# Five changes at once in a layer's forward and backward pass: the filter's transform, the D term, column tiles, the order of the start and of the stage boundaries

## Chip, cores and metric

One core of a Trainium2 chip. The metric is the device time of one execution in microseconds (us). Medians are quoted with their lowest and highest run. Profiles are of single executions.

## The reference, cut to what matters

One layer over a sequence of 2048 rows of 1024 channels, all in bf16, and its gradients with regard to nine inputs:

```python
def _A_ref(q, k, v, shift_k, ssm_k, ssm_D):
    ...                                   # k_shift: 4-tap causal filter of k along the sequence
    kv = k_shift * v
    ...                                   # zero-padded to 4096 rows
    y_f = kv_f * kf_f                     # spectra of kv and of the long filter ssm_k
    y = irfft(y_f)[:S]                    # the long convolution
    y = y + kv * ssm_D                    # the D term
    return q * y

def _B_ref(x, w_gate, w_up, w_down):
    return ((x @ w_gate) * (x @ w_up)) @ w_down      # 1024 -> 3584 -> 1024

xn = layernorm(x)
out = x + _A_ref(xn, k, v, ...) * silu(_B_ref(xn, ...))
# outputs: out, and the vector-Jacobian products for x, k, v, shift_k, ssm_k, ssm_D, w_gate, w_up, w_down
```

## The kernel before

TensorE does the matrix products and also the convolution's Fourier transforms, as products with tables of 128 x 128. The convolution runs beside the big products: it is a generator of small steps ("units of work") that a pump advances after each block of the big products. There are six stages: layer norm (with the first two weight slabs); gate/up products with the forward convolution; bilinear output with the gate; dh and dWgate/dWup with the backward convolution; dWdown; dx with the gradient of k (dk).

The filter's transform took four tables and 64 matmuls per block of 128 channels, and the D term was added in time (two passes of VectorE over a block):

```python
    def fwd2(x, X, wp, psp):                    # radix 2: 4 x 2 x (4 x 2) matmuls of 256 columns
        for q in range(4):
            psS = psp.tile([P, 2, 256], F32, name="psS")
            psP = psp.tile([P, 2, 256], F32, name="psP")
            cmm(psS, T4[q], x, (0, 2, 4, 6))
            cmm(psP, T4[q], x, (1, 3, 5, 7))
            ...
            tt(X[:, 2 * q:2 * q + 2, :], s[:], psP[:], ADD)
            tt(X[:, 2 * q + 8:2 * q + 10, :], s[:], psP[:], SUB)
    ...
        def main(ds):                           # one block of 128 channels, forward
            ...
            yield from fwd4(kvs, KX, cs, ps_cv)             # kv already in radix 4
            yield from fwd2(S_["hx"], HX, cs, ps_cv)        # the filter
            tt(kvD[:], kvs, Dbc[...], MUL)                  # D term
            yield from product(KX, HX, KX, cs, False, 0)
            yield from inv_dft(KX, HX, cs)
        def tail(ds):
            ...                                             # 4 x inv_rows, ScalarE copies to yf
            tt(yf[:], yf[:], kvD[:], ADD)
```

The gradients of D and of the short filter need only the diagonal of a product, and took the whole product:

```python
            for b in range(NB):                 # D: 16 matmuls of 128 columns
                nc.tensor.matmul(ps[:, 0, :], x[:, b, :], kv[:, b, :], ...)
    ...
            for r in range(8):                  # dk: 8 matmuls of 512 columns, twice per channel block
                nc.tensor.matmul(ps[...], dk[:, r, :], kh[:, r:r + 4, :], ...)
```

The start, PSUM shares of the fourth stage, and its first lines:

```python
    slabs = [load_slab(0, nc.scalar)[0]]
    chunks = [(0, 2), (2, 2), (4, 4), (8, 4), (12, 4)]      # row blocks normed together
    ...
    ps_b = pool("ps_b", 4, space=PSUM)      # dh and dW
    ps_c3 = pool("ps_c3", 1, space=PSUM)    # transforms of dy
    ps_y = pool("ps_y3", 2, space=PSUM)     # rows of the inverse transforms
    ...
    flush()                                 # the gate's last transposes of dbm, ahead of dh
    first = dh_half(0, wdt)
```

Who issues what will matter: SyncE issues most loads, among them the transposed ones (`wdt`, `dgut`, the gate and up weights); ScalarE issues the stores of dWgate, dWup (`out_dram<-wb`) and of `DGd`, and it is also the engine that copies dh and dW out of PSUM (`dht`, `wb`); GpSimd issues the convolution's transfers.

## Time and profile before

| | kernel before |
|---|---|
| time, three runs | 2095.99 us (2095.94 to 2096.73) |
| span of its profile | 2084.4 us |
| TensorE busy | 96% |
| VectorE busy | 70%; 89% in the fourth stage |

The execution that was profiled took 2086.3 us, 10 less than the three runs. In a line of waits, the first name is the engine that waited and the group it then ran, after the arrow stands what ended the wait, then the sum in us, the number of times and the longest. In a timeline line the columns are start, length, engine, line, operation, tiles, count, and in brackets the idle time just before with its cause; "ACTq" and "SPq" are the issuing of a transfer by ScalarE and SyncE.

### The profile page before, as it was taken

The page shows a single profiled execution, that of the slowest core. Times are in us where ns is not written, and L with a number is a line of the kernel's source. Part 1 is how long each engine was busy: PE and PEld are TensorE (multiplying, and loading weights), DVE is VectorE, ACT ScalarE, POOL GpSimd, SP SyncE. Part 2 cuts the span into 40 slices and gives each one's busy share as a digit, 9 for nine tenths or more (in the row PEclk, how much of TensorE's full clock was granted, in tenths as well). Part 3 has the DMA queues.
Part 4 walks back from the last instruction along what each step waited for, and adds up shares of the span by engine and source line. Part 5 has one row for each costly group of instructions (what it writes and reads, how often), then busy time and mean ns, then how long its engine had stood idle before and what let it go on. Part 6 is the DMA issues. An engine that isn't in the chain of part 4 may idle for free.

```text
span 2084.4 us, 28857 instructions
## 1 busy us (share of the span) xinstructions
PE 2001.6 (96%) x11438; PEld 1088.1 (52%) x11626; DVE 1464.0 (70%) x1937; ACT 626.5 (30%) x969; POOL 339.9 (16%) x496
## 2 busy tenths in 40 slices
PE   7989999999999998999899999999999989999998
PEld 3455555555544446666556555565444434444443
DVE  7689898878726555787799999999697024344433
ACT  6734444444423333232122222222222101111112
POOL 3322222121112111000112212111121001110100
PEclk9999999999999999999999999999999999999999
DMA  8776676566598779666878888857954999393921
GB/s 292 241 256 205 220 234 250 186 214 241 178 309 271 246 239 322 212 209 162 257 232 273 242 221 263 246 199 248 253 196 145 236 191 221 96 211 91 225 69 57
DMA packets 454279, 451.29 MB, mean 217 GB/s; under 512 B 236944, under 2 KB 380600, under 8 KB 439680
## 3 DMA queue, kind: packets, MB, share of 16 engines
q1 hardware_dynamic: 308096, 185.89, 34.4%
q0 software_dynamic: 45120, 189.08, 26.8%
q10 hardware_dynamic: 100928, 74.47, 11.7%
q8 instruction: 91, 1.49, 0.3%
q14 instruction: 44, 0.36, 0.1%
HBM read 208.15 MB, written 194.02 MB: 193 GB/s over the span
## 4 chain that ended last, share of the span: by engine, by line
PE 42%; DVE 9%; issue 6%; DMA 2%; SPq 2%; POOL 1%; ACT 0%; another core or an unknown queue 0%; ACTq 0%; DVEq 0%; POOLq 0%
PE psx L1212 17%; PE psb L1101 9%; PE psb L1181 9%; PE psb L1082 4%; DVE W L199 3%; DVE m L199 2%; SPq L1152 1%; PE psdk L939 1%; DVE U L199 1%; DMA dyl<-DYd 1%; DMA B<-HFd 1%; DVE B L199 1%; PE psY L904 1%; DVE B L242 0%; SPq L1206 0%
## 5 line engine op out<-in xcount | busy, mean ns | idle before, releaser
L1101 PE MATMUL psb<-U,U 128*128 128x512 bf16 x1746 | 400.4, 383 | 9.5 <-ACT dht L1084 4.2
L567 PE MATMUL psg<-wslab,U 128*128 128x512 bf16 x1729 | 402.5, 380 | 4.2 <-ACT gut L569 0.7
L1212 PE MATMUL psx<-U,dgut 128*128 128x512 bf16 x1508 | 336.2, 380 | 7.4 <-DMA dgut<-DGd 5.8
L1212 PEld LDWEIGHTS <-dgut 128*128 128x128 bf16 x1792 | 175.5, 98 | 219.2 <-DMA dgut<-DGd 7.2
L1101 PEld LDWEIGHTS <-U 128*128 128x128 bf16 x1792 | 176.6, 99 | 210.2 <-issue 15.9
L567 PEld LDWEIGHTS <-U 128*128 128x128 bf16 x1792 | 173.4, 98 | 187.3 <-issue 4.6
L1082 PE MATMUL psb<-wdt,U 128*128 128x256 bf16 x1792 | 205.5, 274 | 0.0
L569 ACT CAST gut<-psg 128x512 bf16<-128x512 f32 x224 | 130.9, 585 | 218.6 <-PE psg L567 215.8
L1181 PE MATMUL psb<-U,U 128*128 128x512 bf16 x875 | 194.9, 379 | 1.1
L1082 PEld LDWEIGHTS <-U 128*128 128x128 bf16 x1792 | 176.2, 98 | 23.1
L964 PE MATMUL psbm<-U,ht 128*128 128x512 bf16 x766 | 170.4, 379 | 1.4 <-DMA ht<-HTd 0.4
L1105 ACT CAST wb<-psb 128x512 bf16<-128x512 f32 x112 | 65.5, 585 | 324.0 <-PE psb L1101 236.9
L199 DVE TENSOR_TENSOR W<-W 128x1024 f32<-128x1024 f32 (+1 forms) x144 | 146.1, 1033 | 2.7
L199 DVE TENSOR_TENSOR m<-A,B 128x1024 bf16<-128x1024 bf16 (+1 forms) x160 | 116.6, 791 | 37.2 <-issue 21.6
L1181 PEld LDWEIGHTS <-U 128*128 128x128 bf16 x896 | 87.0, 98 | 102.1
L1235 ACT ACTIVATE dx_t<-dxn 128x1024 bf16<-128x1024 f32 (+1 forms) x17 | 17.1, 1007 | 362.0 <-DVE dxn L199 310.8
L964 PEld LDWEIGHTS <-ht 128*128 128x128 bf16 x784 | 76.0, 98 | 89.7 <-DMA ht<-HTd 0.9
L199 DVE TENSOR_TENSOR dka<-dkh,Wbc 128x1024 bf16<-128x1024 bf16 x16 | 11.1, 692 | 156.6 <-DMA dkh<-DKSHd 156.6
L1084 ACT CAST dht<-psb 128x512 bf16<-128x512 f32 x112 | 65.1, 587 | 144.8 <-PE psb L1082 102.7
L199 DVE TENSOR_TENSOR U<-U,dht 128x2048 bf16<-128x2048 bf16 x56 | 71.6, 1282 | 18.5 <-ACT dht L1084 18.5
L1183 ACT CAST U<-psb 128x512 bf16<-128x512 f32 x56 | 32.8, 585 | 159.8 <-PE psb L1181 131.2
L199 DVE TENSOR_TENSOR gg<-bm,sig 128x1024 bf16<-128x1024 bf16 x16 | 11.1, 691 | 92.0 <-ACT sig L982 92.0
(239 smaller groups left out, 2473.9 us busy)
## 6 DMA issues: line engine op xcount, KB each, us to landing
U<-GUd SPq DMA_DIRECT2D x28, 1024.0 KB, 7.4
DGd<-U ACTq DMA_DIRECT2D x56, 512.0 KB, 5.7
GUd<-gut ACTq DMA_DIRECT2D x54, 512.0 KB, 4.6
A<-DYFd POOLq DMA_DIRECT2D x16, 1024.0 KB, 7.5
U<-Hd SPq DMA_DIRECT2D x15, 1024.0 KB, 6.1
out_dram<-wb ACTq DMA_DIRECT2D x224, 64.0 KB, 2.9
Hd<-hN POOLq DMA_DIRECT2D x54, 256.0 KB, 4.6
HTd<-hT POOLq DMA_DIRECT2D x54, 256.0 KB, 3.6
```

Of the source, the lines that this page charges most:

```text
L199: V.tensor_tensor(o, a, b, op)
L567: gu_mm[0] = nc.tensor.matmul(ps[:], XNT[q][:, dc, qi * P:(qi + 1) * P], w[:, dc].rearrange("p a f -> p (a f)"), start=(dc == 0), stop=(dc ...
L569: nc.scalar.copy(out=gut[:, i].rearrange("p a f -> p (a f)"), in_=ps[:])
L904: nc.tensor.matmul(ps[:, i, :], G[:, 2 * r + k, c * P:(c + 1) * P], TI[:, 0, r, k, :], start=(k == 0), stop=(k == 1))
L964: nc.tensor.matmul(ps[:, dh * 512:(dh + 1) * 512], ht(fc)[:, i * P:(i + 1) * P], WD[fc // 4][:, fc % 4, dh * 512:(dh + 1) * 512], start=(f ...
L1082: nc.tensor.matmul(ps[:, x * SLW:(x + 1) * SLW], DBMT[2 * hf + g][:, dc, (b % 4) * P:(b % 4 + 1) * P], wdt[:, dc, :], start=(dc == 0), sto ...
L1084: nc.scalar.copy(out=dht[:, 2 * e:2 * e + 2].rearrange("p b f -> p (b f)"), in_=ps[:])
L1101: nc.tensor.matmul(ps[:], XN[b // 4][:, b % 4, dc * P:(dc + 1) * P], dgus[b // 8][:, b % 8].rearrange("p a f -> p (a f)"), start=(b == 0), ...
L1105: nc.scalar.copy(out=wb[:].rearrange("p a f -> p (a f)"), in_=ps[:])
L1181: nc.tensor.matmul(ps[:], h[:, b, f * P:(f + 1) * P], DBM[b // 4][:, b % 4, dh * 512:(dh + 1) * 512], start=(b == 0), stop=(b == NB - 1))
L1183: nc.scalar.copy(out=wbs[:, dh * 512:(dh + 1) * 512], in_=ps[:])
L1212: nc.tensor.matmul(ps[:, dh * 512:(dh + 1) * 512], t[n][:, f, i * P:(i + 1) * P], WGU[n][:, f, dh * 512:(dh + 1) * 512], start=(n == 0 and ...
```

## The change

Its intent is to take work off TensorE (filter transform in radix 4: 32 matmuls in place of 64; diagonals by two column tiles of 64), work off VectorE (the D term becomes one small addition to the filter's spectrum; its passes in the forward and backward tails go), and holes off the boundaries (smaller first chunks; the last transposes of dbm behind the first dh half; transposed tiles for dx loaded during dWdown). Cut to its core:

```diff
-    T4 = [TF[:, 0], TF[:, 1], TFO[:, 0], TFO[:, 1]]
+    T4 = [TF[:, 0], TF[:, 1]]
...
-            yield from fwd2(S_["hx"], HX, cs, ps_cv)
+            yield from fwd4(S_["hx"], HX, cs, ps_cv)
             turned(HX, 1, 0, 1)
+            h0 = cv(HX[:])[:, :, 0, 0]
+            tt(h0, h0, Dbc[:, ds * P:(ds + 1) * P].unsqueeze(1).to_broadcast([P, 8, P]), ADD)
-            tt(kvD[:], kvs, Dbc[...].to_broadcast([P, NB, P]), MUL)
...
-            tt(yf[:], yf[:], kvD[:], ADD)
...                                    (W gets a second buffer in the forward pass)
-            flush(2)
+            flush(3)                   (transposes of hN one row block later)
...
-    slabs = [load_slab(0, nc.scalar)[0]]
-    chunks = [(0, 2), (2, 2), (4, 4), (8, 4), (12, 4)]
+    chunks = [(0, 1), (1, 1), (2, 2), (4, 4), (8, 4), (12, 4)]
...                                    (slab 0 on SyncE's queue, behind the first chunk)
-                nc.tensor.matmul(ps[:, 0, :], x[:, b, :], kv[:, b, :], ...)
+                for j in (slice(0, 64), slice(64, 128)):
+                    nc.tensor.matmul(ps[j, 0, 0:64], x[:, b, j], kv[:, b, j], ...)
...
-        tt(dy[:], dy[:], Dbc[...], MUL)
-        tt(y[:], y[:], dy[:], ADD)
...
-                nc.tensor.matmul(ps[:]..., dk[:, r, :], kh[:, r:r + 4, :]..., ...)
+                for j in (slice(0, 64), slice(64, 128)):
+                    nc.tensor.matmul(ps[j], dk[:, r, j], kh[:, r:r + 4, j], ...)
...
-    C_TOTAL = ... + 8 * 5.4 + 8 * 0.5     (pace of the backward convolution)
+    C_TOTAL = ... + 8 * 2.9 + 8 * 0.5
...
-    ps_b = ... 4;  ps_c3 = ... 1;  ps_y = ... 2
+    ps_b = ... 3;  ps_y = ... 1;  ps_c3 = ... 2, replaced by ps_y4 = ... 4 after the dy transforms
...
-    flush()
+    for e in later:
+        e[0] = -2
...
-    HSL = (3, 11, 6, 2)                   (tiles of h in dWdown: four)
+    HSL = (3, 11, 6)                      (three)
...                                    (nine weight tiles, as before, and now nine dgut tiles loaded during dWdown)
```

## The prediction

> **What bounds the kernel now.** I read the busy table first, then busy time by stretch (the stages cut where the big matmul groups begin and end), then the waits of each stretch. The columns of a stretch are its length, then busy time and instruction count of TensorE, its weight loads, VectorE, ScalarE and GpSimd, then clock and DMA.
>
> ```profile
> PE 2001.6 (96%) x11438; PEld 1088.1 (52%) x11626; DVE 1464.0 (70%) x1937; ACT 626.5 (30%) x969; POOL 339.9 (16%) x496
> ```
> ```profile
> 0.00:93.00 93.00, 78.90 (x490) 39.93 (x500) 67.09 (x158) 64.81 (x91) 28.55 (x51) 1.00 0.78 259
> 93.00:584.00 491.00, 472.96 (x3003) 278.32 (x3055) 408.65 (x518) 224.56 (x351) 107.51 (x163) 1.00 0.66 223
> 584.00:790.00 206.00, 200.32 (x1004) 94.52 (x1024) 106.41 (x168) 63.99 (x64) 39.35 (x62) 1.00 0.85 273
> 790.00:1450.00 660.00, 633.08 (x4026) 390.72 (x4073) 586.60 (x730) 172.34 (x302) 99.10 (x142) 0.98 0.77 235
> 1450.00:1653.00 203.00, 201.78 (x1039) 96.76 (x1058) 131.06 (x151) 42.74 (x77) 26.98 (x18) 1.00 0.82 207
> 1653.00:2084.40 431.40, 414.53 (x1882) 187.80 (x1918) 164.15 (x214) 58.08 (x86) 38.41 (x61) 0.99 0.65 149
> ```
>
> The reader is to see six stages (layer norm; gate/up products with the forward convolution; bilinear output with the gate; dh and dWgate/dWup with the backward convolution; dWdown; dx with dk) and TensorE near full in all. VectorE has room except in the fourth stage and, at 83%, the second. So TensorE bounds the time, and anything taken off it counts, unless VectorE steps in.
>
> The chain of waits shows that the busy matmuls are at their own rate:
>
> ```profile
> 1713.39 10.74 PE psx L1212 x49
> ```
>
> (10.74 - 0.38)/48 = 0.216 us from start to start, 0.38 being the last one's own duration in the table of groups. Time can therefore only come from fewer columns streamed or from the holes. The holes that concern the change:
>
> ```profile
> PE psb L1003 <- DVE dbm L199: 6.7, 1, 6.7
> PE psY L407 <- DVE B L199: 4.3, 1, 4.3
> PE psb L1101 <- ACT dht L1084: 4.2, 1, 4.2
> PE psY L407 <- ACT yl L882: 3.8, 1, 3.8
> ...
> PE psx L1212 <- DMA dgut<-DGd: 5.8, 3, 3.5
> ```
>
> The first four are in the fourth stage (the first is its very beginning), the last is the start of dx.
>
> **What the Trainium skill says.** "TensorE: Matmul & The Clock Gate", section "Back-to-back issue gap": a warm matmul of N columns follows the last after N/2.4 + 2.5 ns: 215.8, 109.2 and 55.8 ns for 512, 256 and 128. The trace agrees (0.216 us above; runs of 128-column transposes start 0.056 us apart). "TensorEngine Tiling (Array Packing)", section "Key Properties": column tiles work in parallel, but a change of tiling mode drains the array; its section "Restrictions" says column tiling turns the fast weight load off. The kernel before never tiles, so no trace here shows either. "VectorE: DVE Perf Modes", section "Side-by-side": two-input 16-bit operations reach two results a cycle, fp32 one; the trace agrees: 512 fp32 elements take 682 ns, 1024 bf16 elements 682 ns.
>
> **The change part by part.**
>
> (1) *Filter transform in radix 4, D in the spectrum.* The old transform of the filter takes 64 matmuls of 256 columns for each of 8 column blocks, the new one 32, as the transform of kv has. Removed: 256 x 0.1092 = 28.0 us of TensorE, all in stage 2. VectorE pays. Its groups (union of time, 8 blocks):
>
> ```profile
> L199 DVE TENSOR_TENSOR HX<-Ws,psP 128x512 bf16<-128x512 f32 x64 | 40.8, 682 | 20.2 <-PE psP L216 20.1
> L199 DVE TENSOR_TENSOR W<-W,psP 128x512 f32<-128x512 f32 x64 | 40.4, 682 | 14.7 <-ACT W L229 13.8 <-PE psP L216 0.6
> L199 DVE TENSOR_TENSOR KX<-W 128x512 bf16<-128x512 f32 x64 | 39.8, 683 | 0.0
> L199 DVE TENSOR_TENSOR kvD<-kv,Dbc 128x2048 bf16<-128x2048 bf16 x8 | 9.8, 1224 | 0.2
> L199 DVE TENSOR_TENSOR yf<-yf,kvD 128x2048 bf16<-128x2048 bf16 x8 | 9.8, 1222 | 18.2 <-ACT yf L670 18.0
> ```
>
> The first row goes, a second copy of rows two and three comes: +80.2 - 40.8 = +39.4. Rows four and five go: -19.6. The new addition of D to the spectrum is 8 operations of 1024 bf16, 0.64 each: +5.1. Net +24.9 us. Now the stage by its two engines. TensorE ideal before: 1536 products of 512 columns x 0.2158 + 512 transposes x 0.0558 + 1024 of kv, filter and inverse x 0.1092 = 472, against 491 measured; after: 444. VectorE before had 405 of its 409 us done when the last block's inverse ended, at 565.6; TensorE had waited 1.4 us for it there and needed 20 us more (the convolution is paced to end at 95% of the stage). After: 405 + 25 = 430 us. It also stands still for loads of k that no part of the change hastens (14.3 us in this stage before):
>
> ```profile
> DVE U L199 <- DMA k<-KSLd: 14.3, 4, 6.7
> ```
>
> I allow 6 us for other waits; the 18.0 for yf go with the operation, and most of the 13.8 for W with its second buffer, which the freed tables pay for. So the inverse ends 450 us after 93, and the stage 20 later, at 563 instead of 584: **-21 us, not -28**, because VectorE becomes the bound of this stage.
>
> (2) *Start.* First chunk of one row block, not two: the first transposes began at 11.0 us; two statistics (0.67 each), an aggregate and two scalings (0.48 each) less ahead of them make 2.5 us, an earlier landing about 1; two of four table builds go too, beside other work. **-4.**
>
> (3) *Gate to dh.* The deferred transposes of the last block now stand behind the first dh half, 64 matmuls of 256 columns = 7.0 us, in TensorE's order, as the two programs' orders show. They fill the hole of 6.7: **-7.**
>
> (4) *Backward.* The tail of each of 8 units loses two operations of 1.22 us and a load of 0.5 MB: 19.5 us of VectorE. Between 1000 and 1250 us TensorE lost about 17 us to waits of which VectorE, 95 to 99% busy, is the cause. The first 6.6, at the turn from the dy transforms to the products, come from a load that must wait for buffers (VectorE waits 9.3 us for B from HFd) and stay; of the rest I take 7, plus 2 for the four PSUM buffers of the rows. Against it: dh and dW have three PSUM buffers, not four (+1), and the D gradient's 128 matmuls of 128 columns (7.1 us) become 256 of 64 columns. At that size the floor per instruction and the slower weight load leave nothing of the parallelism, and 16 switches of mode at an estimated 0.17 us each (one unhidden passage of the array, the 166 ns that the matmul page's section "Single matmul latency" has above the streaming) cost 2.7: +4. **-4 net.**
>
> (5) *dWdown to dx.* 9 of 14 pairs of transposed tiles are loaded before dx begins; the five weight loads left need 4 to 7 us each on the queue (they did at 1652 to 1696), some 25 us, and the tenth pair is wanted 9 x 16 x 0.2158 = 31 us into the stage. The 5.8 us of idle, with the shorter waits around it about 7.5 us against the ideal rate, go: **-7.5.**
>
> (6) *dk by column tiles.* 128 matmuls of 512 columns take 27.6 us in a stage where TensorE never rests. As 128 pairs of 256 columns, if the halves run side by side, a pair takes 0.109 to 0.14; I take 0.125: 16.0 us, plus 32 switches x 0.17 = 5.4. **-6.** If they do not, 256 x 0.109 + 5.4 = 33 us, +6.
>
> Sum: -21 - 4 - 7 - 4 - 7.5 - 6 = -49.5 on 2096.0, about 2047.
>
> **The rivals.**
> - *VectorE hands back the whole gain of stage 2.* For it: 430 us of work by 450 us into the stage is 96% busy, in order, tied to ScalarE and TensorE. Against: it ran at 97% from 1050 to 1450, and stage 2 gains a second W buffer. At 90% the inverse would end at 93 + 478 = 571 and the stage at 591, 28 above my figure: 2075.
> - *Stage 2 stays TensorE's.* Then the full 28 us, plus the 7.8 us that the transposes of hN waited and that the longer deferral removes: 15 us better, 2032. VectorE's k loads speak against it.
> - *Column tiles run one after the other* because of weight loads or drains: +12 on my sum, 2059.
> - *The backward stalls only move*, from dy to the load of v, which has small rows and shares one queue: +7, 2054.
>
> **Range and chances.** Spreads of about 9 (stage 2), 6 (backward), 6 (tiles), 2 (start), 2 (boundaries) make 13 together. Range 2030 to 2064. Two per cent is 2054, about half a spread above 2047: faster 0.69, same 0.30, slower 0.01; every part but the VectorE exchange takes work or holes away from the bound.
>
> **What would show it.** Stage 2 (first matmul of slab 2 to first of the bilinear output) 470 us long with VectorE above 90%; no wait of TensorE for dbm at the start of dh and none for dgut at the start of dx; blocks of 16 dk matmuls lasting about 1.3 us in place of 1.73; waits of TensorE for B, dht and yl under 10 us in stage 4; first transpose before 8 us. Wrong would be: VectorE idle and TensorE waiting for psS, psP or HX all through stage 2; dk blocks at 2 us; a new wait for dht because of three PSUM buffers.

## The result, and the profile after

| | before | after |
|---|---|---|
| time, four runs each on one chip | 2095.97 us (2091.29 to 2096.73) | 2061.59 us (2059.75 to 2063.34) |
| span of the first profile | 2084.4 | 2061.4 |

The ratio is 0.984, with a 95% interval of 0.9822 to 0.9859: faster by 1.6%, which is under 2%, so that the class is "same". (Ratios here are the mean time of one kernel's fast runs over that of the other's of the same rounds, so not quite the ratio of the medians that are quoted.) The figure lies in the predicted range, 14.6 us above the predicted one, and in the class that had been given 0.30.

The stretches of the kernel after, cut where its big groups of matmuls begin (the columns are those of the prediction's table):

```profile
0.00:93.00 93.00, 76.22 (x449) 37.24 (x450) 67.77 (x165) 58.18 (x86) 30.03 (x53) 0.98 0.71 243
93.00:578.70 485.70, 457.24 (x2858) 257.56 (x2857) 428.22 (x576) 223.70 (x353) 107.97 (x164) 0.99 0.67 229
578.70:784.15 205.45, 200.95 (x1020) 94.21 (x1018) 105.74 (x167) 63.73 (x64) 39.26 (x62) 1.00 0.85 272
784.15:1444.87 660.72, 631.40 (x4201) 387.88 (x4201) 568.27 (x720) 171.94 (x302) 95.30 (x134) 0.99 0.76 229
1444.87:1647.95 203.08, 203.08 (x1068) 96.99 (x1066) 119.63 (x145) 43.38 (x77) 26.23 (x18) 1.00 0.81 214
1647.95:2061.40 413.45, 404.02 (x2040) 186.08 (x2038) 159.78 (x214) 57.52 (x86) 38.53 (x61) 0.99 0.65 151
```

VectorE is busy for 428 us in the second stretch, as foretold (430), but the stretch is 486 us long where 470 was foretold; the fourth did not shrink; the last did, by more than its part of the sum. A single profile of each kernel is a thin base, so each kernel was profiled a second time (runs x_before and x_after below). Stage lengths in us, both profiles of each, by the same cuts; the start ends with the 33rd copy of a gate/up product out of PSUM, which is the first after the layer norm's chunks:

| stage | before | after | mean difference | predicted |
|---|---|---|---|---|
| start | 92.0, 92.5 | 99.4, 98.3 | +6.6 | -4 |
| rest of gate/up | 493.5, 494.1 | 479.3, 478.7 | -14.8 | -21 |
| bilinear, to first dh | 210.9, 210.6 | 205.4, 204.5 | -5.8 | -7 |
| dh, dWgate/dWup | 653.7, 660.6 | 660.7, 650.1 | -1.8 | -4 |
| dWdown | 203.5, 213.7 | 203.1, 203.1 | -5.5 | 0 |
| dx, dk | 430.8, 434.5 | 413.5, 421.5 | -15.2 | -13.5 |
| span | 2084.4, 2106.0 | 2061.4, 2056.1 | -36.5 | -49.5 |

The last two stages carry -7.5 (dgut) and -6 (dk) in the prediction. The two profiles of one kernel agree within 1.1 us in the first three stages and differ by up to 11 in the later ones.

**The granted clock.** Neither the prediction nor the table names it. It stands at 1.00 but for stretches of 3.4 us, or a few times that, in which it is 0.50 and matmuls of 512 columns start 0.427 us apart, not 0.216. In the first profiles of both kernels each such stretch, the one behind the last matmul aside, lies in a hole of TensorE of 2 us or more or within 4 us behind one, so that a hole can cost more than its own length. The dx stage of x_after shows it (a line of the timeline, and one of busy time by stretch, its third figure from the end the clock):

```profile
1844.59 8.75 PE L1211 MATMUL psx<-U,dgut 128*128 128x512 bf16 x28 [5.36 <-DVE dxn L202]
```
```profile
1844.60:1849.80 5.20, 5.20 (x13) 1.85 (x13) 2.59 (x3) 3.51 (x5) 0.00 (x0) 0.50 1.05 222
```

A hole of 5.4 us and half of the 5.2 us behind it make the 8.0 us by which this stage is longer than in the first profile of the kernel after. The two first profiles have 30.7 us of such stretches each, so the clock is no part of the difference between them; x_before has 44.4, x_best 68.3.

**The start.** The first transposes begin 3.2 us earlier, the first product only 0.8. TensorE in the kernel before:

```profile
11.00 1.89 PE L542 MATMUL tr<-ident,x 128*128 128x128 bf16 x16 [11.00 <-DVE x L539]
13.14 4.12 PE L567 MATMUL psg<-wslab,U 128*128 128x512 bf16 x13 [0.25 <-ACT U L543]
```

TensorE, then ScalarE, in the kernel after:

```profile
7.81 1.03 PE L531 MATMUL tr<-ident,x 128*128 128x128 bf16 x8 [7.81 <-DVE x L528]
12.34 1.03 PE L556 MATMUL psg<-wslab,U 128*128 128x512 bf16 x2 [3.49 <-ACT U L532]
```
```profile
11.18 0.20 ACT L507 ACTIVATE r__229<-vpe 128x1 f32<-128x1 bf16 x1 [5.14 <-DVE vpe L505]
11.29 0.99 ACT L532 COPY U<-tr 128x1024 bf16<-128x1024 bf16 x1
...
23.39 0.59 ACT L558 CAST gut<-psg 128x512 bf16<-128x512 f32 x1 [3.71 <-DMA GUd<-gut]
```

ScalarE's copy of the first transposes stands in its list behind the square root of the second chunk, and starts 0.1 us after it began, though the transposes had ended at 8.8 us: the second chunk's statistics are on the first chunk's path. The last line is the other cost: a chunk of one row block fills a whole `gut` tile, there are two of these, and each is free only when its store has landed. A third is small: TensorE waits 1.7 us at 96.9 us for the load of the third weight slab (not at all before, 1.1 in x_start below).

**Gate/up.** First VectorE's waits in the gate/up stage after, then TensorE's:

```profile
DVE U L202 <- DMA k<-KSLd: 28.3, 5, 11.7
DVE hN L202 <- ACT gut L558: 18.5, 6, 7.4
DVE W L202 <- ACT W L232: 9.2, 8, 2.4
```
```profile
PE tr L570 <- DVE hN L202: 16.8, 10, 6.5
PE psP L219 <- DVE W L202: 7.1, 6, 2.6
PE psY L407 <- DVE HX L202: 2.3, 4, 1.0
```

VectorE's waits for yf and for psP are gone (18.0 and 20.7 us before) and those for W fell from 13.8 to 9.2, but its waits for k doubled (14.3 before), and so did TensorE's for VectorE: 26.2 us against 12.8 (7.8 for hN, 2.8 for W, 2.2 for HX). From the 49th copy on, summed over start times and not over busy time, TensorE's own work fell by 24.5 us (seven of eight filter transforms) and its holes grew from some 14 to 27 us (the first estimated, since 50 records of that part are missing there, at 0.2158 us each).

**Gate to dh.** The hole of 6.7 us for dbm is gone, and another is there:

```profile
791.58 8.90 PE L1071 MATMUL psb<-wdt,U 128*128 128x256 bf16 x80
805.52 1.06 PE L792 MATMUL psY<-kvx,dyx 128*64 128x64 bf16 x32 [5.04 <-DMA kvx<-KVd]
```

From the last bilinear matmul to the first of dW it is 33.3 us before and 36.4 after (33.4 and 33.6 in the second profiles).

**dh and dW.** TensorE's waits there:

```profile
PE psb L1071 <- ACT dht L1073: 5.0, 3, 3.5
PE psY L396 <- DVE B L246: 4.7, 2, 4.1
PE psb L1090 <- ACT dht L1073: 3.7, 3, 2.0
PE psb L1090 <- ACT wb L1094: 3.3, 2, 1.9
```

The waits for B and yl of before (11.3 us with all groups) are down to 4.7; waits for ScalarE's copies (dht, wb), 4.2 us for dht before, are up to 12.0. Why ScalarE is late is one of the questions below.

**dx.** The wait for dgut is gone. A piece of dk in a stage where TensorE never rests:

```profile
1665.22 1.89 PE L1211 MATMUL psx<-W,dgut 128*128 128x512 bf16 x8
1667.05 0.52 PE L928 MATMUL psdk<-kh,dkh 128*64 128x256 bf16 x6
1667.50 0.82 PE L1211 MATMUL psx<-W,dgut 128*128 128x512 bf16 x3
```

Six tiles, three pairs, occupy 0.45 us from their start to the next group's. By the start times of all of them (medians): the second of a pair starts 3 ns after the first, the next pair 106 ns later, so that a pair takes 109 ns, which is the rate of one matmul of 256 columns; the step into a run of tiles takes 309 ns in place of 216, the step out of it 205 in place of 106. A change of mode costs 0.093 to 0.099 us here.

### The profile page after: what moved, and what is told of

Read it like the earlier page. It is cut to its first block, busy times and chain, and to the rows that moved or that the text cites. A ratio compares the mean times of both kernels' runs of the same rounds, so it can differ in the third digit from the quotient of the medians.

```text
span 2061.4 us, 29060 instructions
## 1 busy us (share of the span) xinstructions
PE 1972.9 (96%) x11626; PEld 1060.0 (51%) x11626; DVE 1449.4 (70%) x1985; ACT 618.4 (30%) x966; POOL 337.3 (16%) x491
## 3 DMA queue, kind: packets, MB, share of 16 engines
q1 hardware_dynamic: 310320, 186.94, 34.6%
## 4 chain that ended last, share of the span: by engine, by line
PE 57%; DVE 18%; issue 14%; DMA 6%; POOL 2%; ACT 1%; ACTq 0%; SPq 0%; POOLq 0%; DVEq 0%
PE psx L1211 19%; PE psb L1188 9%; PE psb L1090 9%; PE psbm L952 8%; DVE W L202 5%; DVE m L202 5%; PE psg L556 4%; PE psb L1071 3%; DVE HX L202 2%; DVE U L202 1%; DMA k<-KSLd 1%; DMA B<-HFd 1%; DVE KX L202 1%; DVE A L202 1%; PE psdk L928 1%
## 5 line engine op out<-in xcount | busy, mean ns | idle before, releaser
L556 PE MATMUL psg<-wslab,U 128*128 128x512 bf16 x1792 | 416.6, 383 | 7.0 <-ACT U L532 4.9
L1211 PEld LDWEIGHTS <-dgut 128*128 128x128 bf16 x1792 | 173.9, 98 | 210.9 <-issue 3.4
L558 ACT CAST gut<-psg 128x512 bf16<-128x512 f32 x224 | 131.2, 586 | 231.9 <-PE psg L556 218.8
L202 DVE TENSOR_TENSOR W<-W,psP 128x512 f32<-128x512 f32 x128 | 80.6, 681 | 9.2 <-ACT W L232 9.2
L1190 ACT CAST wbs<-psb 128x512 bf16<-128x512 f32 x56 | 32.8, 586 | 159.5 <-PE psb L1188 151.0
L202 DVE TENSOR_TENSOR U<-U,dht 128x2048 bf16<-128x2048 bf16 x56 | 68.3, 1220 | 17.0 <-ACT dht L1073 17.0
```

The costliest lines, as they stand in the source:

```text
L202: V.tensor_tensor(o, a, b, op)
L556: gu_mm[0] = nc.tensor.matmul(ps[:], XNT[q][:, dc, qi * P:(qi + 1) * P], w[:, dc].rearrange("p a f -> p (a f)"), start=(dc == 0), stop=(dc ...
L558: nc.scalar.copy(out=gut[:, i].rearrange("p a f -> p (a f)"), in_=ps[:])
L1190: nc.scalar.copy(out=wbs[:, dh * 512:(dh + 1) * 512], in_=ps[:])
L1211: nc.tensor.matmul(ps[:, dh * 512:(dh + 1) * 512], t[n][:, f, i * P:(i + 1) * P], WGU[n][:, f, dh * 512:(dh + 1) * 512], start=(n == 0 and ...
```

## The experiments

Each is the kernel after with one edit, unless said otherwise. "Before" is the kernel before on the same chip in the same rounds. Several chips served, and the times of one kernel spread more than in the first runs (the kernel before: 2082 to 2108).

| run | edit | median us (range, n) | before us | ratio, 95% | start / gate-up / bilinear / dh-dW / dWdown / dx |
|---|---|---|---|---|---|
| x_before | kernel before | 2107.9 (1) | 2089.5 | | 92.5 / 494.1 / 210.6 / 660.6 / 213.7 / 434.5 |
| x_start | old start | 2058.6 (2055.1-2065.3, 4) | 2089.5 | 0.9835 (0.9787-0.9884) | 93.6 / 479.5 / 206.5 / 658.0 / 208.9 / 413.5 |
| x_k | copies of k earlier | 2074.1 (2066.6-2078.9, 4) | 2089.5 | 0.9906 (0.9863-0.9949) | 100.8 / 478.8 / 205.6 / 667.9 / 209.7 / 414.2 |
| x_k2 | and two buffers for k, v | 2063.3 (2059.5-2078.7, 4) | 2089.5 | 0.9872 (0.9821-0.9923) | 103.5 / 472.0 / 204.8 / 665.1 / 203.1 / 413.4 |
| x_psum | old PSUM shares | 2074.8 (2062.8-2093.9, 4) | 2098.0 | 0.9881 (0.9828-0.9934) | 98.0 / 479.9 / 204.6 / 671.0 / 216.7 / 421.9 |
| x_spq | dW stores on SyncE | 2069.7 (2062.2-2082.2, 4) | 2098.0 | 0.9882 (0.9837-0.9926) | 98.6 / 479.5 / 204.2 / 654.1 / 210.3 / 413.7 |
| x_notiles | no column tiles | 2076.0 (2070.8-2077.8, 4) | 2098.0 | 0.9902 (0.9873-0.9930) | 100.0 / 480.2 / 204.4 / 658.0 / 203.2 / 423.1 |
| x_radix2 | filter in radix 2 | 2092.4 (2088.4-2100.0, 4) | 2098.0 | 0.9989 (0.9955-1.0022) | 98.5 / 502.4 / 204.1 / 667.3 / 203.1 / 422.9 |
| x_flush | dbm ahead of dh | 2074.9 (1) | 2084.7 | | 99.6 / 479.9 / 210.8 / 657.1 / 212.3 / 413.5 |
| x_late | backward convolution later | 2093.4 (1) | 2084.7 | | 99.3 / 480.1 / 204.3 / 688.8 / 204.7 / 414.5 |
| x_after | none | 2061.4 (2057.9-2080.8, 6) | 2087.7 | 0.9890 (0.9856-0.9924) | 98.3 / 478.7 / 204.5 / 650.1 / 203.1 / 421.5 |
| x_best | four edits | 2085.9 (2081.0-2092.6, 6) | 2087.7 | 0.9988 (0.9965-1.0011) | 94.7 / 478.6 / 204.4 / 652.3 / 231.9 / 417.4 |

All results were correct. The profiled run of x_psum is slow (2093.9); its other three runs are fast.

**x_before: the kernel before once more.**

> The kernel before, unchanged, for a second profile. The first profile of it spans 2084.4 us, while its three timed runs lie at 2096; the changed kernel's profile (2061.4) is as long as its runs. So the two profiles differ by 23.0 us and the medians by 34.4. Theory: the profiled run of before was a quick one (its other runs spread by 5 us), and the missing ten microseconds sit in one or two stages whose waits vary from run to run; a second profile should be 2088 to 2096 long and show in which stage: I expect the stage of the backward convolution (653.7 us from the first dh matmul to the first dWdown matmul). Rival: the profiler itself makes the kernel before quicker by 10 us, and the second profile is again near 2084.

The profile was not 2088 to 2096 but 2106.0 us long. Each of the first three stages repeats within 0.6 us; dh/dW is 6.9 us longer, dWdown 10.2, dx 3.7. So the first half is a firm measure and the second is not; the rival (the profiler makes it quicker) falls. This run's extra holes are waits for ScalarE's copies dht and yl.

**x_start: the old start.**

```diff
-    chunks = [(0, 1), (1, 1), (2, 2), (4, 4), (8, 4), (12, 4)]
+    slabs = [load_slab(0, nc.scalar)[0]]
+    chunks = [(0, 2), (2, 2), (4, 4), (8, 4), (12, 4)]
```

> The changed kernel with only the old beginning: first chunk of two row blocks, first weight slab on ScalarE's queue at once, products of the broadcast two chunks in. Theory: the one-block chunks cost more than they give, since every small chunk pays a whole wait for one of two gut buffers (3.7 and 3.3 us) and ScalarE's copy of the first transposes stands behind the square root of the second chunk; so the 33rd gut copy ends near 91.4 us as in the kernel before and not at 98.9, and the time falls by 5 to 8 us against the changed kernel's 2061.6, to 2054 to 2057. Rival: the gate and up products are paced by VectorE after that, so a quicker start is waited away; the end of the gate/up products stays at 578 us and the time within 2 us of 2061.6. Second rival, my own prediction: the new start was worth 4 us, and undoing it makes the time 2066.

The start takes 93.6 us in place of 99.4, the last gate/up copy ends at 571.9 in place of 577.5: 5.6 of the 5.8 us are kept to the end of that stage, so the first rival and my own prediction both fall. The gain of the total is not shown by the times (2058.6, but the ratio's interval is wide); dWdown lost 6 us in the profiled run to a wait for a tile of h, told below.

**x_k and x_k2: VectorE's waits for k.**

```diff
+        if i == 3:                     # in the start (x_k2: i == 2)
+            copy_k(1)
-        if sl in (2, 4, 7):  copy_k({2: 1, 4: 2, 7: 3}[sl])
+        if sl in (3, 6):     copy_k({3: 2, 6: 3}[sl])
```

x_k2 besides:

```diff
-            v = U[4][:, 0:2048]...;  k = kst.tile([P, 2, 11, P], BF16, name="k")
+            v = U[4][:, 2048 * c:2048 * c + 2048]...;  k = kst.tile(..., name="k", bufs=2)
-                nx = 2 * dp + c + 1
+                nx = 2 * dp + c + 2
```

> The changed kernel with the DRAM copies of k issued earlier: the second pair's behind the first pair's in the start, the third's and fourth's one slab earlier. Theory: the 11.7 us that VectorE waited for k between 99 and 111 us come from the second copy, issued at 87 and landed at 100 us, and are on the path, because VectorE is 94% busy from there to the end of the stage; the wait there falls to about 3 us, VectorE's waits for k in this stage from 28.3 to about 19, and the time by 5 to 9 us, to 2053 to 2057. Rival: the earlier copies (1 MB) delay the loads of the start by some 4 us and the gain is lost: time 2058 to 2063, the 33rd gut copy later than 98.9 us. The second large wait, 11.5 us at 352, should stay, since it comes from the order of GpSimd's queue.

> As the run before, and besides the tiles of k and v have two buffers, so that each half pair is loaded a half pair ahead. Theory: VectorE's waits for k in the gate/up stage fall from 28.3 us to under 5, VectorE ends the forward convolution 20 us or more sooner, and since the stage is VectorE's the gate/up products end at 558 to 566 us in place of 578.7: time 2040 to 2049. Rival: TensorE becomes the bound before that; it has 444 us of work in this stage by its own rate and took 486, and waits for hN and for the start's chunks stay: then the gain is half, 8 to 12 us, time 2050 to 2054. Second rival: k was never on the path (TensorE's waits are for ScalarE and gut), and the time stays within 3 us of 2061.6 although the waits for k go.

The theory falls in both. In x_k the wait near 105 us fell from 11.7 to 6.9, but others grew, and VectorE's waits for k were 31.9 us in all in place of 28.3; the last gate/up copy came 0.9 later. In x_k2 the waits for k are gone, yet the last copy came only 3.2 us sooner. Two things are hidden in that figure. The start, in which the copies of k now lie, took 4.1 us longer than in the kernel after. And from the 33rd to the 49th copy it took 37.6 us in place of 46.3 (40.5 in x_k), so the first wait for k, near 105 us, was on the path, and the start and what followed gave most of it back. From the 49th copy on nothing was won: 433.1 us against 431.8. One reason is in VectorE's waits of x_k2:

```profile
DVE U L202 <- DMA KSHd<-U: 16.2, 3, 6.6
```

The tile in which the shifted k is summed is the next thing that is not free: it must first be stored. The wait moved from a load to a store. TensorE's waits for VectorE, from the 49th copy on, are 19.4 us there against 18.2 in the kernel after. Behind the first slab the loads of k were not what sets the stage's length; for the time, the second rival of x_k2 (within 3 us) is what came. The larger time of x_k (2074) is not shown to be the edit's: its profile lost 7 us in dh/dW and 7 in dWdown, which the edit doesn't touch.

**x_radix2: the filter's transform undone alone.**

```diff
-            yield from fwd4(S_["hx"], HX, cs, ps_cv)
+            yield from fwd2(S_["hx"], HX, cs, ps_cv)      # four tables again, one buffer for W
```

> The changed kernel with the filter's transform in radix 2 again (D still in the spectrum; one buffer for W, since the second table takes its memory). It adds 28 us of matmuls and takes 39 us off VectorE in the gate/up stage. Theory: TensorE lost 28 us of work there and won 12 to 13 us of waits for VectorE, so undoing it lengthens the stage by 10 to 16 us: last gut copy at 587 to 593 us in place of 576.9, TensorE's waits for W and hN back from 16 us to about 6; time 2072 to 2078. Rival: in the changed order nothing hides the 28 us, the last gut copy comes at 600 or later, time 2085 or more. Second rival: VectorE was the whole bound, and giving it 39 us back makes the stage no longer at all (577 to 582).

The last gate/up copy came at 591.9, which is 14.4 us later than in the kernel after; from the 33rd copy on, 493.4 us in place of 478.1. That is the theory's 10 to 16. The time rose by more. In the profile 8.7 us are lost after that copy, where 1.4 were in the kernel after; dh/dW is 6.6 us longer (a hold of ScalarE, see x_late) and dx 9.4, of which 7.2 are one wait for VectorE. As to the 8.7: VectorE's list has an operation of the gate, which waits for a load, ahead of the last product hN that TensorE waits for:

```profile
598.64 0.69 DVE L204 TENSOR_TENSOR so<-xn_t,yf_t 128x1024 bf16<-128x1024 bf16 x1 [13.36 <-DMA yf_t<-YFd]
599.25 0.68 DVE L204 TENSOR_TENSOR hN<-gut 128x1024 bf16<-128x1024 bf16 x1
```

These 7.3 us are an accident of that order, not the transform's worth. As to the mechanism, TensorE's waits for W, 7.1 us in the kernel after, do not occur at all here, with 39 us less on VectorE and 28 more on TensorE; those for hN, which the theory also counted, stay at 9.3 without the last one (8.8 in the kernel after). The filter's transform is worth 14 to 15 us in this stage; D in the spectrum was not undone by itself.

**x_notiles: the column tiles undone.**

```diff
-                for j in (slice(0, 64), slice(64, 128)):
-                    nc.tensor.matmul(ps[j], dk[:, r, j], kh[:, r:r + 4, j], ...)
+                nc.tensor.matmul(ps[:]..., dk[:, r, :], kh[:, r:r + 4, :]..., ...)     # D's gradient likewise
```

> The changed kernel without column tiles: dk's and D's gradients with full-width diagonals as before. Theory, from the traces: a pair of 256-column tiles takes 0.126 us and the switches show nothing, so dk gives back 11.6 us (stage of dx from 413.4 to 424 to 426) and D's gradient 1.7 in the backward stage; time 2071 to 2077. Rival, the prediction: each run of tiles pays 0.17 us for each change of mode, so dk is worth 6 and D's gradient costs 4; then the time rises by 2 only, to 2062 to 2066.

The dx stage is 423.1 us, 9.6 longer than in the first profile of the kernel after. Start times say the same: 128 matmuls x 0.216 = 27.6 us against 128 pairs x 0.109 + 34 changes x 0.096 = 17.2. Seven profiles with tiles have 413.4 to 414.5 us there; the four with more (417.4 to 422.9) have waits for VectorE (dxn) of 2.6 us or more that x_notiles has not. The ratios cannot tell (0.990 here, 0.989 in x_after on another chip). So the theory is right in its sum and wrong in a detail: the switches do show, at 0.09 to 0.10 us each. D's gradient is 7.1 us at full width and about 5.6 in tiles (128 pairs x 0.031 = 4.0, and 16 changes of about 0.1). The prediction's version (+2 in all) falls.

**x_flush: the transposes of dbm ahead of dh again.**

```diff
-    for e in later:
-        e[0] = -2
+    flush()
```

> The changed kernel with the last block's transposes of dbm ahead of the first dh half again, as before. Theory: the change took away the hole of 6.7 us for dbm, but the same time came back at once: in the changed kernel TensorE waits 5.0 us for kvx, 2.1 for Ws and 1.6 for W before its first dW matmul, because it now reaches the D gradient before the loads of kvx and dyx have landed. So with the old order the hole of 6 to 7 us for dbm is back, the wait for kvx goes, and the first dW matmul comes 34 to 37 us after the last bilinear matmul, as in the changed kernel (36.4): the term is worth 0 to 2 us. Rival, the prediction: the wait for kvx stays as it is and the hole comes on top, 42 to 44 us, so that the term was worth its 7.

```profile
789.39 1.04 PE L991 MATMUL psb<-ident,dbm 128*128 128x128 bf16 x8 [6.70 <-DVE dbm L202]
...
808.56 0.69 PE L792 MATMUL psY<-kvx,dyx 128*64 128x64 bf16 x32
```

The hole is back, the wait for kvx is gone (it stood at 4.1 to 6.0 us in every profile with the new order and the old pace), and the first dW matmul comes 33.9 us after the last bilinear one. Ten profiles with the new order and the old pace have 31.9 to 36.6, mean 34.3. The theory holds: TensorE reached the next thing that was not ready sooner by what it had saved.

**x_late: the backward convolution begun later.**

```diff
-        bpump((bcnt[0] - 8) / (BT - 8))
+        bpump((bcnt[0] - 12) / (BT - 12))          # and kvx loaded ahead of dyx
```

> The changed kernel with the backward convolution begun four ticks (one dh half, 7 us) later and with the load of kvx issued ahead of that of dyx. Theory: the wait for kvx (5.0 us) goes and with it the stumbling after it; the first dW matmul comes 29 to 32 us after the last bilinear matmul, in place of 36.4, and the first dWdown matmul 4 to 7 us sooner, if nothing later takes it back. Rival: the transfers are the bound there (the DMA engines are 99% busy), dyx or wdt become the wait, and the first dW matmul stays at 35 to 38 us; or the later convolution ends later and its rows make TensorE wait for B in the dWdown stage, which then grows beyond 203 us.

The wait for kvx went, and the first dW matmul came after 24.9 us, partly because convolution work now lies behind it. But the dh/dW stage was 688.8 us long. Its one large hole, TensorE's wait and ScalarE's time in issuing:

```profile
PE psb L1090 <- ACT wb L1094: 39.5, 1, 39.5
```
```profile
1003.84 47.23 ACTq L68 DMA_DIRECT2D DGd<-U  x2
```

ScalarE, which must empty PSUM, stood for 47.2 us in the issue of two stores. At this point, near 1005 us, the convolution turns from the transforms of dy to the products, GpSimd sends off loads of 1 MB each, SyncE a transposed load of Wdown (21.3 us in its own issue), and the DMA engines are 99% busy while they move only 40 to 130 GB/s. The longest hold of ScalarE between 996 and 1050 us, by run: 8.4 and 7.6 (two profiles of before), 10.9 and 6.5 (two of after), 3.4 (x_spq), 11.4, 11.5, 13.1, 13.5, 18.4 (x_radix2), 19.8 (x_k), 21.9 (x_psum), 47.2 here. What a hold costs can be read off: with three PSUM buffers, TensorE's longest wait for wb is the hold less 8.9 to 9.0 us in all seven profiles that have one and whose hold is in these stores (13.5 costs 4.5, 19.8 costs 10.8), and holds of 3.4 and 6.5 cost nothing. That is a large part of the spread of the dh/dW stage, not all of it: x_k2 has 665.1 us with a hold of 11.4. Which of the transfers does the holding was not isolated. Whether the later beginning itself is a gain stays open.

**x_psum: the fourth PSUM buffer.**

```diff
-    ps_b 3, ps_y 1, ps_c3 2, ps_y4 4
+    ps_b 4, ps_y 2, ps_c3 1, ps_y4 2
```

> The changed kernel with the PSUM shares of the backward stage as before: four buffers for dh and dW, one each for the dy transforms' sums, two for the rows. Theory: in the changed kernel ScalarE stands in its own store issue for 61 us of this stage (28 before), once 10.9 us, and three PSUM buffers bridge only some 10 us of matmuls (3.45 us each) where four bridge 14; so TensorE's waits for dht and wb (12.0 us) fall to about 6, and the stage from first dh to first dWdown matmul, 660.7 us, to 653 to 657; time 2053 to 2058. Rival: the fourth buffer's gain is given back, since the dy transforms and the rows have half the buffers; the stage stays within 3 us of 660 and the time within 3 us of 2061.6.

Inconclusive for the time: the runs spread from 2062.8 to 2093.9, and the profiled one is slow. Its hold was 21.9 us:

```profile
PE psb L1090 <- ACT wb L1094: 9.4, 1, 9.4
```

With four buffers 12.5 us of it were bridged, with three 8.9 to 9.0 in seven profiles (listed under x_late). The difference fits a buffer's 3.45 us, but four buffers show it in a single profile, which is slow; whether the fourth buffer outweighs what the rows gained is not settled either.

**x_spq: the stores of dW away from ScalarE.**

```diff
-            sta(o_dwg[...], wb[:, 0, :]);  sta(o_dwu[...], wb[:, 1, :])      # wb: 4 buffers
+            ld(o_dwg[...], wb[:, 0, :]);   ld(o_dwu[...], wb[:, 1, :])       # wb: 8 buffers
```

> The changed kernel with the stores of dWgate and dWup issued on SyncE's queue, not on ScalarE's, and eight wb tiles in place of four, so that ScalarE never stands in the issue of a store of weights. Theory: the waits of TensorE for dht and wb in this stage (12.0 us in the changed kernel, up to 10.8 in one wait in another run) come from ScalarE being held in its issue, because it is the engine that empties PSUM; they fall to 3 to 5, the stage from 660.7 to 650 to 655 us, the time to 2051 to 2056. Rival: SyncE's queue is in order and holds transposed loads of up to 20 us in front of the stores, and the tile loads for the next slab behind them; then new waits of TensorE for wdt or U appear and the stage is as long or longer (660 to 670).

TensorE's waits for wb are gone and those for dht are 7.9 us in all, against 12.0 for both; the dh/dW stage takes 654.1 us. That is the theory's figure, but 3 to 5 us of waits had been foretold, and the unchanged kernel's second profile has no wait for wb either, 7.2 for dht and a stage of 650.1. The time (ratio 0.988) is no better than that of the kernel after. So neither the fall of the waits nor a gain in time is shown to come from the edit; what the profile shows is a short hold (3.4 us).

**x_after and x_best.** The second joins four edits: the old start, `flush(4)` for the transposes of hN, all stores of the fourth stage on SyncE, and this one:

```diff
-            hs[k + 1] = load_h(k + 1, HSL[(k + 1) % 3])
+            hs[k + 1] = load_h(k + 1, HSL[(k + 1) % 3], sta)      # h for dWdown on ScalarE's queue
```

> The changed kernel, unchanged, on the chip of the next run: a base for it, and a second profile. Theory: its length varies from run to run with one collision of transfers at about 1010 us, where the first loads of the backward products, a transposed load of Wdown and ScalarE's stores meet (ScalarE was held 7.6 to 8.4 us there in two profiles of before, 10.9, 13.5, 11.4 and 19.8 in four with the changed order, and 47.2 in one), and with a wait of 4 to 6 us for a tile of h in the dWdown stage that was absent in its first profile; so I expect a median of 2060 to 2070 here, a ratio to before of 0.982 to 0.990. Rival: 2059.8 to 2063.3 as in the first five runs, and the same holes as in the first profile within 1 us.

> Four edits together: the old beginning, the transposes of hN held back one block longer, all stores of the fourth stage on SyncE's queue with eight wb tiles, the loads of h for dWdown on ScalarE's queue. Theory: the start gives 5.5 us, the waits for hN (8.8 us) halve, ScalarE is never held by a store, so TensorE's waits for dht and wb (12 us and more) fall to 4, and the wait for h in dWdown (4 to 6 us in most runs) goes: 14 to 22 us below the run of the changed kernel on the same chip, 2040 to 2048, ratio to before 0.972 to 0.980. Rival: SyncE's queue now holds stores that wait for VectorE's products in front of loads, and new waits for wdt or for the gate and up products take most of it back: 5 us or less below the changed kernel.

x_after: the median is 2061.4 again, one run of six at 2080.8, and the ratio is 0.989, so the theory's figures came. Its profile has the hold at 6.5 us and no wait for wb, and instead 5.4 us of another wait in dx: the rival (the same holes within 1 us) falls. It does not have the wait for h in dWdown. That wait had 3.6 to 6.6 us in the profiles of x_start, x_k, x_spq and x_flush, 2.5 in x_psum and 1.5 in x_late: a load of h comes late in some runs. Likely causes are the three tiles of h in place of four and the transposed loads placed closer together on the same queue; neither was undone alone.

x_best failed, by 24 us against x_after on the same chip, and the profile tells where. Start 94.7, dh/dW 652.3: as hoped. Gate/up 478.6, no gain from the longer deferral; TensorE's waits there, from the 49th copy on:

```profile
PE psP L219 <- DVE W L202: 11.7, 8, 3.0
PE psY L407 <- DVE HX L202: 6.3, 7, 2.0
PE tr L570 <- DVE hN L202: 1.8, 2, 0.9
```

With the wait for hN cut from 8.8 us (in the same part of the kernel after) to 1.8, those for W and HX rose from 9.4 to 18.0: the sum is 19.8 against 18.2. TensorE waits for VectorE as such, at whichever place comes first. And dWdown is 231.9 us long. ScalarE there, then SyncE:

```profile
1495.45 1.07 ACT L1189 CAST wbs<-psb 128x512 bf16<-128x512 f32 x2 [28.36 <-DMA out_dram<-wbs]
```
```profile
1443.13 34.55 SPq L1146 DMA_TRANSPOSE U<-in_B_w_gate_dram  x1
1477.77 14.39 SPq L1146 DMA_TRANSPOSE U<-in_B_w_up_dram  x1
```

SyncE stood in the issue of these two transposed loads for 34.6 and 14.4 us (7.4 and 10.1 for the same two in the kernel after); the stores of dWdown behind them were late, and ScalarE, out of `wbs` tiles, left PSUM full. Why the issue took so long is not isolated. Taking the loads of h off SyncE's list did not bring the first of the two much closer to the one before it (0.7 us, where the kernel after has 1.2); what else differs is that two loads of h, 1 MB each, ran beside it on ScalarE's queue, and the DMA engines moved 182 GB/s from 1443 to 1478 us, against 290 in the kernel after from 1455 to 1475. No version beat the kernel after with certainty; the old start alone is the one edit with a gain that the profile shows and nothing against it.

## Why the prediction was right, and where it missed

It had the range right and the centre 15 us too low. That the figure fell inside is in part luck: the range is 34 us wide, and the errors of the steps have both signs (see the sum below). By its own steps:

1. **Filter transform and D in the spectrum, -21: the mechanism right, the size too large; -15.** The 28 us of TensorE went, and VectorE took part of them back, as said. VectorE's work was foretold well too: 426 us from 93 us to the end of the last block's inverse on VectorE, against 430. The failed term is the time it needs for that work: 450 us were assumed (20 of waiting), it took 469 (562 less 93), 43 of them waiting, 91% busy; some 7 of the 19 too many are the late start. The end at 562 lies between the 543 of the prediction and the 571 of its first rival, and the stage ended 16 us later, not 20. VectorE's waits for k had been taken as the 14.3 us of before; they were 28.3, but the experiments show that past the first slab k was not what counted (x_k, x_k2), and that TensorE's waits for VectorE move from place to place with nearly the same sum (x_best) and lose the W part when VectorE has less to do (x_radix2). The 91% is what came out in this stage and this order, and no general limit: VectorE ran at 97% from 1050 to 1450 us in the kernel before. The pump also fixes where the steps of the convolution stand among the big products (the last rows end 8.8 to 9.1 us before the last copy in all eleven profiles with the new transform), and another pace was not tried, so how much of the waiting is owed to the order stays open.
2. **Start, -4: wrong; +6.6.** The step that failed is the assumption that the chunk's shorter work is all there is to its path. The first transposes did start 3.2 us earlier, the first product 0.8, and after that the small chunks lost. ScalarE's order and the two gut buffers show in the trace; x_start, which also puts the first slab's load back on ScalarE's queue, shows the price (5.8 us), not the share of each.
3. **Gate to dh, -7: the hole went, the gain did not stay; 0.** Foretold was only that the transposes fill the hole. That the next piece of work would then come before its loads (5.0 us for kvx) was not thought of. x_flush shows both halves.
4. **Backward, -4: not to be told from nothing.** The stage is 657.2 us before and 655.4 after, as means of two profiles that lie 7 and 11 apart. The sign set for it, waits for B, dht and yl under 10 us, failed: 13.4 in the first profile. Of its terms, D's gradient in tiles was put at +4, since nothing of the parallelism was to be left at this size, and is about -1.5: a pair of 64 columns takes 31 ns, a matmul of 128 columns 56; the waits for B and yl fell by 6.6, those for dht and wb rose by 7.8 in the first profile. "A new wait for dht because of three PSUM buffers" had been named as what would show the step wrong; the cause is wider: ScalarE held in its own issue; that three buffers bridge less of it than four is likely from x_psum, where one profile stands against seven.
5. **dWdown to dx, -7.5: right.** No wait for dgut; with the column tiles undone, the dx stage is 423.1 us against 430.8, 7.7 less. Before, the hole of 5.8 us is followed by 3.4 us at half clock, which is 1.7 more and fits the prediction's "shorter waits around it". Not foreseen was that the loads moved into dWdown can cost 4 to 6 us there in some runs.
6. **dk in tiles, -6: right in kind, too small; -10.** The pair was put at 0.125 us and is 0.109, and a change of mode at 0.17 and is 0.096: 17.2 us in place of 21.4.

The sum of the table is -36.5 in place of -49.5: +10.6 from the start, +6.2 from the filter, +3.4 from the gate and the backward stage, less 1.7 in dx and 5.5 in dWdown, of which the last comes from one long profile of the kernel before.

## What to carry to other kernels

When two engines alternate in order, a gain on one can be paid back through the other's waits before either is full: do not count on more than what that stage shows already, and when a wait is removed, ask what the engine reaches next and whether that is ready. Count a hole of TensorE with the stretch at half clock behind it. An engine that empties PSUM and also issues transfers can be held in their issue (up to 47.2 us here), and so can a queue of transposed loads (34.6 us): look at what stands behind them in the list before moving anything there. Profile each kernel twice before explaining a stage: here two profiles agreed within 1.1 us in one half and differed by up to 11 in the other.

## What the Trainium skill lacked or had wrong

- "TensorEngine Tiling (Array Packing)", section "Key Properties", says that a change of tiling mode drains the array and gives no price. Here a step into a run of 64-column tiles took 309 ns in place of 216 and a step out of it 205 in place of 106, over 34 such changes: 0.093 and 0.099 us, about half of the estimate made from the array's passage. That two tiles work in parallel is borne out: a pair of 256 columns takes 109 ns.
- "TensorE: Matmul & The Clock Gate", section "Wait — 56ns, not 53.3ns?", has start-to-start never below about 25 ns, while its section "Measured speedup vs the span model" has about 4 ns for each further tile; the page does not say that the first figure leaves out tiles that run together. Here the second of a pair starts 3 ns after the first, in line with the 4, and pairs of 64 columns follow each other by 31 ns, 15.5 ns a matmul, below the 25.
- "DMA: Bandwidth & Descriptors", section "Rules for kernel authors", says that a transpose next to ordinary DMAs needs nothing. That is about correct results, and all results here were correct. What the page lacks is how long the issuing engine can be held: the issue of one transposed load took up to 34.6 us (x_best), and ScalarE's issue of two ordinary stores, begun while one stood in SyncE's issue, 47.2 us (x_late), with the DMA engines 99% busy at 40 to 130 GB/s for most of it.
